# Attention with chunk selection and an MLP: preparing uniform blocks of 256 tokens over all eight heads, in wide instructions, instead of one head pair over the whole sequence

## The chip, the cores and the metric

One core of a Trainium2 chip runs the whole program. The metric is the device time of one execution in microseconds (us). The engines are named as the profile names them: PE (TensorE, matmuls; PEld is its weight load), DVE (VectorE), ACT (ScalarE), POOL (GpSimd) and SP (SyncE, which issues transfers). PSUM is the memory into which this program's matmuls write. SWDGE means the transfers that GpSimd issues, X the MLP's input for one block of tokens.

Every kernel was run beside the kernel before on the same chip, in rounds.

## The reference

Batch 4, 8 heads, 768 tokens, head size 64. Keys are cut into chunks of 32 tokens. For each query an upper bound of its score with every chunk is computed from the chunk's smallest and largest key per dimension; the best six chunks are kept, and causal softmax attention runs over those. Its output, 3072 tokens by 512, goes through an MLP with a softplus.

```python
k_min, k_max = k_chunks.min(axis=3), k_chunks.max(axis=3)
ub = sum(maximum(q * k_min, q * k_max), axis=-1)          # per query and chunk
top_chunks = argsort(where(causal, ub, -1e9))[..., -6:]
scores = where(selected & causal, scale * q @ k.T, -1e9)
attn_out = softmax(scores) @ v                            # 4 x 8 x 768 x 64
h = x @ w_in                                              # 3072x512 @ 512x2048
out = softplus(h) @ w_out                                 # 3072x2048 @ 2048x512
```

## The kernel before

The unit of preparation is a head pair over all 768 tokens, 16 of them. `prep_pair` transposes k and q on PE, reduces each chunk of keys to its maximum and minimum on DVE, computes the bounds `ub` on PE, takes the best of them with one MAX8 instruction per tile and head, and transposes the mask. It is a generator with four pieces, and a piece is emitted at certain slots of the attention of the pair before.

```python
kT = ps_t.tile([128, S], BF16, name="kT", tag="t")
for t in range(NQT): nc.tensor.transpose(kT[:, t*128:(t+1)*128], k_sb[:, t], ident)
nc.vector.tensor_reduce(kx[:, 0], kT3, axis=AX.X, op=ALU.max)     # 768 columns
nc.vector.tensor_reduce(kx[:, 1], kT3, axis=AX.X, op=ALU.min)
nc.scalar.copy(ka[0:64, :], kT[0:64, :]); nc.scalar.copy(kb[64:128, :], kT[64:128, :])
...                                                               # (cut) bd copies, on POOL later
PREP_AT = (0, 1, 4, 8)
for i in range(len(pairs)):                 # 4 batches x 4 head pairs
    nxt = prep_pair(i + 1)
    for blk in range(NBLK):                 # 3 blocks of 256 queries
        for _ in score_step(i, blk):        # 2, 4, 6 slots
            slot([nxt] if idx in PREP_AT else [])
```

A slot emits one score step (two matmuls `s_ps` and one exp `pt`), one step of the attention output that is waiting (`o_ps`, then `rec` and `o_sb` on DVE, which divide by the softmax sum, then the transpose `oT` and the copy into the MLP's input), and one piece of the MLP. The MLP's first matmul writes `hp`, ACT makes the softplus from it (`e_sb`, then `g`), and the second matmul writes `y`. A piece is 8 `hp` matmuls or 4 `y` matmuls, 0.87 us of PE. There is a single `o_ps` buffer in PSUM: the next pair's output can't start before DVE has read the last one.

```python
def av_step(i, blk, pt):
    o_ps = ps_o.tile([128, 2, 2, D + 1], F32, name="o_ps")        # ps_o: bufs=1
    ...
    nc.vector.reciprocal(rec, o_ps[:, :, :, D:D + 1])
    nc.vector.tensor_tensor(o_sb, o_ps[:, :, :, 0:D], rec.to_broadcast(...), op=ALU.mult)
```

The MLP of 256 tokens needs all four head pairs of that block. With this order of loops it becomes possible only in the fourth pair. The order within an engine is not the order of the text: the compiler's scheduler plans it.

The softmax here doesn't subtract the row's maximum and nothing guards it: scores larger than these inputs give would overflow.

Of the kernel before, what the change touches and what calls it, by code (L numbers as in the profile page):

```python
# [14 lines left out]
ACT = mybir.ActivationFunctionType  # L15


@with_exitstack
def kernel(
# [9 lines left out]
    nc = tc.nc  # L29
# [10 lines left out]
    NTOK = B * S  # L40
    KDM = d_model // 128
    KFF = d_ff // 128
    QB = 256
    NBLK = S // QB
    NK = 4
    NV = 5

    nc.scalar.preload_act_table_set("natural_log_exp_and_others")
# [3 lines left out]
    f_pool = ctx.enter_context(tc.tile_pool(name="f", bufs=4))  # L52
    io_pool = ctx.enter_context(tc.tile_pool(name="io", bufs=3))
    qt_pool = ctx.enter_context(tc.tile_pool(name="qt", bufs=4))
    prep = ctx.enter_context(tc.tile_pool(name="prep", bufs=2))
    pt_pool = ctx.enter_context(tc.tile_pool(name="pt", bufs=3))
    st_pool = ctx.enter_context(tc.tile_pool(name="st", bufs=3))
    g_pool = ctx.enter_context(tc.tile_pool(name="g", bufs=3))
# [7 lines left out]

    v_sb = [singles.tile([128, NQT, 2, D + 1], BF16, name=f"v_{i}") for i in range(NV)]
    KA = [singles.tile([128, S], BF16, name=f"ka_{i}") for i in range(NK)]
    KB = [singles.tile([128, S], BF16, name=f"kb_{i}") for i in range(NK)]
    w_in_sb = singles.tile([128, KDM, d_ff], BF16, name="w_in_sb")  # L70
    w_out_sb = singles.tile([128, KFF, d_model], BF16, name="w_out_sb")
    xT = [singles.tile([128, NTOK], BF16, name=f"xT_{p}") for p in range(NP)]

    pairs = [(b, p) for b in range(B) for p in range(NP)]
    loaded = {}

    def load_f32(i):
        for nm, x in (("k", k), ("q", q)):
            xf = f_pool.tile([128, NQT, 2, D], F32, name="xf")
            b, p = pairs[i]  # L80
            for h in range(2):
                nc.sync.dma_start(out=xf[:, :, h, :],  # L82
                                  in_=x[b, 2 * p + h].rearrange("(t s) d -> s t d", s=128))
            xb = io_pool.tile([128, NQT, 2, D], BF16, name=nm + "_sb")
            nc.scalar.copy(xb, xf)
            loaded[nm, i] = xb

    def load_cast(i):
        for nm, x in (("k", k), ("q", q)):
            xb = io_pool.tile([128, NQT, 2, D], BF16, name=nm + "_sb")  # L90
            b, p = pairs[i]
            for h in range(2):
                nc.gpsimd.dma_start(out=xb[:, :, h, :],  # L93
                                    in_=x[b, 2 * p + h].rearrange("(t s) d -> s t d", s=128))
            loaded[nm, i] = xb

    def load_v(i):
        b, p = pairs[i]
        for h in range(2):
            nc.gpsimd.dma_start(out=v_sb[i % NV][:, :, h, 0:D],  # L100
                                in_=v[b, 2 * p + h].rearrange("(t s) d -> s t d", s=128))
# [3 lines left out]
    load_f32(0)  # L105
    load_v(0)

    cmask = singles.tile([128, NQT, NCH], F32, name="cmask")
    nc.vector.memset(cmask, 0.0)
    nc.gpsimd.affine_select(out=cmask, in_=cmask, compare_op=ALU.is_ge, fill=-1.0e30,  # L110
                            base=0, channel_multiplier=1, pattern=[[128, NQT], [-CH, NCH]])
    ohb = singles.tile([32, S], BF16, name="ohb")
    nc.vector.memset(ohb, NEG)
# [6 lines left out]
    BD = [[singles.tile([128, 2, NCH], BF16, name=f"bd{m}_{i}") for m in range(2)]  # L120
          for i in range(2)]
    Mraw = [singles.tile([128, NQT, 2, 32], BF16, name=f"mraw_{i}") for i in range(2)]
    for i in range(2):
        for m in range(2):
            nc.vector.memset(BD[i][m], 0.0)
        nc.vector.memset(Mraw[i], 0.0)
    for i in range(NV):
        nc.vector.memset(v_sb[i][:, :, :, D:D + 1], 1.0)

    def init_k(i):  # L130
        nc.vector.tensor_copy(KA[i][64:96, :], ohb)
        nc.vector.memset(KB[i][0:32, :], 0.0)
        nc.vector.tensor_copy(KB[i][32:64, :], ohb)

    load_f32(1)
    load_v(1)
    for kt in range(KDM):
        nc.gpsimd.dma_start(out=w_in_sb[:, kt, :], in_=moe_w_in[kt * 128:(kt + 1) * 128, :])

    QA, QT, owner = {}, {}, {}  # L140

    def prep_pair(i):
        ka, kb = KA[i % NK], KB[i % NK]
        kmx, kmn = BD[i % 2]
        mraw = Mraw[i % 2]
        early = i < NP
        if i < NK:
            init_k(i)
        k_sb = loaded.pop(("k", i))
        q_sb = loaded.pop(("q", i))  # L150

        kT = ps_t.tile([128, S], BF16, name="kT", tag="t")
        for t in range(NQT):
            nc.tensor.transpose(kT[:, t * 128:(t + 1) * 128], k_sb[:, t], ident)  # L154
        kT3 = kT.rearrange("d (c g) -> d c g", g=CH)
        kx = prep.tile([128, 2, NCH], BF16, name="kx")
        nc.vector.tensor_reduce(kx[:, 0], kT3, axis=AX.X, op=ALU.max)  # L157
        nc.vector.tensor_reduce(kx[:, 1], kT3, axis=AX.X, op=ALU.min)
        nc.scalar.copy(ka[0:64, :], kT[0:64, :])
        nc.scalar.copy(kb[64:128, :], kT[64:128, :])  # L160
        eng = nc.vector if early else nc.gpsimd
        for m, dst in enumerate((kmx, kmn)):
            for h in range(2):
                eng.tensor_copy(dst[h * 64:(h + 1) * 64, h], kx[h * 64:(h + 1) * 64, m])
        owner["k", i % NK] = i
        yield

        qT = ps_t.tile([128, S], BF16, name="qT", tag="t")
        for t in range(NQT):
            nc.tensor.transpose(qT[:, t * 128:(t + 1) * 128], q_sb[:, t], ident)  # L170
        n = i + 2
        if n < len(pairs):
            if n < NP:
                load_f32(n)
            else:
                load_cast(n)
            load_v(n)
            owner["v", n % NV] = n
        if i == 1:
            for c4 in range(4):  # L180
                nc.gpsimd.dma_start(
                    out=w_out_sb[:, c4 * 4:(c4 + 1) * 4, :],
                    in_=moe_w_out[c4 * 512:(c4 + 1) * 512, :].rearrange(
                        "(kt ki) f -> ki kt f", ki=128))
        qt = qt_pool.tile([128, S], BF16, name="qt")
        qa = qt_pool.tile([128, S], BF16, name="qa")
        qpos = prep.tile([128, S], BF16, name="qpos")
        qneg = prep.tile([128, S], BF16, name="qneg")
        if early:
            nc.scalar.copy(qt, qT)  # L190
        else:
            nc.vector.tensor_copy(qt, qT)
        nc.vector.tensor_scalar_max(qpos, qt, 0.0)
        nc.vector.tensor_scalar_min(qneg, qt, 0.0)
        nc.vector.tensor_copy(qa[0:64, :], qt[0:64, :])
        QA[i], QT[i] = qa, qt
        yield

        ub = ps_t.tile([128, NQT, 2, NCH], F32, name="ub", tag="t")
        for t in range(NQT):  # L200
            ts = slice(t * 128, (t + 1) * 128)
            nc.tensor.matmul(ub[:, t], qpos[:, ts], kmx, start=True, stop=False)
            nc.tensor.matmul(ub[:, t], qneg[:, ts], kmn, start=False, stop=True)  # L203
        ub_sb = prep.tile([128, NQT, 2, NCH], F32, name="ub_sb")
        nc.vector.tensor_tensor(ub_sb, ub,
                                cmask.unsqueeze(2).to_broadcast([128, NQT, 2, NCH]), op=ALU.add)
        m8 = prep.tile([128, NQT, 2, 8], F32, name="m8")
        for t in range(NQT):
            for h in range(2):
                nc.vector.max(out=m8[:, t, h], in_=ub_sb[:, t, h])  # L210
        nc.vector.tensor_tensor(mraw[:, :, :, 0:NCH], ub_sb,
                                m8[:, :, :, TOPK - 1:TOPK].to_broadcast([128, NQT, 2, NCH]),
                                op=ALU.is_lt)
        nc.vector.tensor_copy(mraw[:, :, :, NCH:NCH + 1], m8[:, :, :, 0:1])
        yield

        mT = ps_t.tile([64, S], BF16, name="mT", tag="t")
        for t in range(NQT):
            nc.tensor.transpose(mT[:, t * 128:(t + 1) * 128], mraw[:, t], ident)  # L219
        nc.vector.tensor_copy(qa[64:96, :], mT[0:32, :])  # L220
        nc.vector.tensor_copy(qt[32:64, :], mT[32:64, :])
        yield

    later = deque()
    done = {}
    clock = [0]

    def score_step(i, blk):
        assert owner["k", i % NK] == i
        t0 = 2 * blk  # L230
        pt = pt_pool.tile([128, 2, NQT, QB], BF16, name="pt")
        for h in range(2):
            kk, rows, qq = ((KA[i % NK], 96, QA[i]), (KB[i % NK], 128, QT[i]))[h]
            for j in range(0, t0 + 2, 2):
                last = j == t0
# [37 lines left out]
    def ot_step(i, blk, o_sb):  # L273
        b, p = pairs[i]
        oT = ps_t.tile([128, QB], BF16, name="oT", tag="t")
        for u in range(2):
            nc.tensor.transpose(oT[:, u * 128:(u + 1) * 128], o_sb[:, u], ident)  # L277
# [62 lines left out]
    def slot(piece_gens=()):  # L340
        for g_ in piece_gens:
            next(g_, None)
# [55 lines left out]
```

## Time and profile before

The kernel takes 323.89 us (median of 3 runs, 323.69 to 324.35); the profiled execution spans 322.0 us.

From the page of the kernel before: the span in 40 slices of 8 us, the digit being the busy share in tenths, and the engines on the chain that ended last.

```profile
PE   1213788698999999899999999999999999999984
DVE  5543638957556657668474847484747321200010
ACT  2306756747997978868888888787879787566620
DMA  9999999909373929478392929100000000011001
PE 78%; ACT 7%; SPq 4%; DMA 4%; DVE 3%; issue 2%; POOL 1%; ACTq 0%; POOLq 0%
```

The DMA engines are full up to slice 8 (64 us). PE's digits are low up to 32 us and below nine in most slices up to 80 us (slice 10); from 80 us PE is full until the end. The windows view of the tile `hp` (the first MLP matmul) says it more exactly. Its columns are the stretch, its length, busy time and count of PE and of ACT, then the granted clock of PE (1.00 is full), the busy share of the DMA engines and GB/s.

```profile
0.00:40.00 40.00, 0.61 (x2) 0.00 (x0) 1.00 1.16 170
40.00:90.00 50.00, 9.00 (x67) 4.26 (x8) 0.83 1.01 81
90.00:278.00 188.00, 74.23 (x565) 42.49 (x71) 1.00 0.44 49
```

The MLP hardly exists before 80 us.

Busy time can't price pipelined matmuls (the record of an `hp` lasts 274 ns, but the next one ends 109 ns later), so I count differently, here and below. From the trace's records I take the step from one matmul's end to the next: 109 ns for 256 columns (`hp`), 216 ns for 512 (`y`), 56 ns for a 128-column transpose, 30 ns for `o_ps`, 25 ns for `ub`. The Trainium skill, "TensorE: Matmul & The Clock Gate", section "Wait — 56ns, not 53.3ns?", gives columns / 2.4 GHz plus about 2.5 ns on a warm array, and the first three agree. Steps times counts is 249.9 us of PE work. A stretch's length less the work that ended in it is PE time lost there:

| stretch of the kernel before, us | length | PE work | lost |
|---|---|---|---|
| 0 to 40 | 40 | 5.1 | 34.9 |
| 40 to 90 | 50 | 25.7 | 24.3 |
| 90 to 278 | 188 | 181.6 | 6.4 |
| 278 to 322 | 44 | 37.4 | 6.6 |

### The profile page before, as it was taken

Reading aid. Unit: us, or ns where it says so; the run is one execution under the profiler, and the core shown is the slowest. Engines: PE = TensorE matmul, PEld = TensorE weight load, DVE = VectorE, ACT = ScalarE, POOL = GpSimd, SP = SyncE. Lnnn points to the kernel's source line nnn. Section 1 sums busy time; section 2 is a strip of 40 time slices with the busy share of each in tenths; the row PEclk is TensorE's granted clock in tenths of the full one; section 3 lists DMA queues with packets and bytes.
Section 4 is the critical chain, followed back from the end, with each engine's and each line's share of the span. In section 5 each row is a group of like instructions: output and inputs, shape, how many; then the busy total and the mean of one; then the engine's idle time right before and its main releaser. Section 6 shows DMA issues by size and latency. Waiting matters only on the chain.

```text
span 322.0 us, 7075 instructions
## 1 busy us (share of the span) xinstructions
PE 278.0 (86%) x2784; PEld 203.4 (63%) x2784; DVE 167.9 (52%) x573; ACT 225.0 (70%) x381; POOL 123.9 (38%) x242
## 2 busy tenths in 40 slices
PE   1213788698999999899999999999999999999984
PEld 0102465485867777677777777777777777666631
DVE  5543638957556657668474847484747321200010
ACT  2306756747997978868888888787879787566620
POOL 8401688846444545558191919131212111000000
PEclk9999997857999999999999999999999999999999
DMA  9999999909373929478392929100000000011001
GB/s 151 197 193 184 128 185 106 91 7 70 26 51 49 92 20 88 59 53 85 38 83 44 99 43 71 38 35 34 2 35 35 34 2 35 33 63 37 33 35 67
DMA packets 81442, 21.96 MB, mean 68 GB/s; under 512 B 75776, under 2 KB 77824, under 8 KB 81408
## 3 DMA queue, kind: packets, MB, share of 16 engines
q0 software_dynamic: 65408, 12.06, 46.2%
q1 hardware_dynamic: 16000, 9.44, 10.6%
q8 instruction: 22, 0.36, 0.5%
q14 instruction: 12, 0.10, 0.1%
HBM read 27.26 MB, written 6.29 MB: 104 GB/s over the span
## 4 chain that ended last, share of the span: by engine, by line
PE 78%; ACT 7%; SPq 4%; DMA 4%; DVE 3%; issue 2%; POOL 1%; ACTq 0%; POOLq 0%
PE y L311 26%; PE hp L298 25%; PE o_ps L260 7%; PE s_ps L238 7%; PE s_ps L241 5%; SPq L82 4%; DMA xf<-in_q_dram 4%; ACT pt L243 3%; PE mT L219 3%; PE oT L277 2%; PE kT L154 2%; PE qT L170 1%; ACT e_sb L300 1%; DVE y_sb L316 1%; PE ub L203 1%
## 5 line engine op out<-in xcount | busy, mean ns | idle before, releaser
L243 ACT ACTIVATE pt<-s_ps 128x384 bf16<-128x384 f32 (+1 forms) x192 | 101.3, 548 | 30.0 <-PE s_ps L241 27.9
L311 PE MATMUL y<-w_out_sb,g 128*128 128x512 bf16 x384 | 98.2, 379 | 1.6 <-DVE y_sb L316 1.6
L247 POOL TENSOR_SCALAR_AFFINE_SELECT pt<-pt 128x256 bf16<-128x256 bf16 x96 | 40.1, 426 | 135.7 <-ACT pt L243 134.5
L298 PEld LDWEIGHTS <-w_in_sb 128*128 128x128 bf16 x768 | 70.7, 98 | 12.9 <-issue 1.2
L300 ACT ACTIVATE e_sb<-hp 128x512 f32<-128x512 f32 x96 | 57.5, 600 | 27.5 <-PE hp L298 26.7
L298 PE MATMUL hp<-xT_116,w_in_sb 128*128 128x256 bf16 x192 | 52.4, 274 | 0.8 <-ACT e_sb L300 0.8
L298 PE MATMUL hp<-xT_118,w_in_sb 128*128 128x256 bf16 x192 | 52.4, 274 | 0.0
L298 PE MATMUL hp<-xT_119,w_in_sb 128*128 128x256 bf16 x192 | 52.4, 273 | 0.0
L298 PE MATMUL hp<-xT_117,w_in_sb 128*128 128x256 bf16 x192 | 52.3, 273 | 0.0
L311 PEld LDWEIGHTS <-g 128*128 128x128 bf16 x384 | 34.4, 97 | 27.3 <-issue 2.1
L302 ACT ACTIVATE g<-e_sb 128x1024 bf16<-128x1024 f32 x48 | 50.9, 1060 | 0.4
L316 DVE COPY y_sb<-y 128x512 f32<-128x512 f32 x24 | 16.6, 692 | 51.6 <-PE y L311 51.5
L260 PEld LDWEIGHTS <-pt 128*128 128x128 bf16 x672 | 32.5, 103 | 4.4 <-issue 1.6
L157 DVE TENSOR_REDUCE kx<-kT 128x24 bf16<-128x768 bf16 x16 | 15.3, 958 | 20.6 <-PE kT L154 20.6
L93 POOL DMA_DIRECT2D k_sb<-in_k_dram x24 | 20.1, 839 | 7.1 <-PE kT L154 6.4
L93 POOL DMA_DIRECT2D q_sb<-in_q_dram x24 | 20.6, 861 | 0.8 <-issue 0.6
L154 PE MATMUL kT<-ident,k_sb 128*128 128x128 bf16 x96 | 9.3, 242 | 13.4 <-ACT kb_110 L160 7.1
L268 DVE TENSOR_TENSOR o_sb<-o_ps,rec 128x256 bf16<-128x256 f32 x48 | 20.1, 419 | 1.1
L266 DVE RECIPROCAL rec<-o_ps 128x4 f32<-128x4 f32 x48 | 8.4, 176 | 22.9 <-PE o_ps L260 22.6
L220 DVE COPY qa<-mT 32x768 bf16<-32x768 bf16 x16 | 8.8, 549 | 16.7 <-PE mT L219 16.6
L277 PE MATMUL oT<-ident,o_sb 128*128 128x128 bf16 x96 | 14.2, 232 | 2.0 <-DVE o_sb L268 2.0
L154 PEld LDWEIGHTS <-k_sb 128*128 128x128 bf16 x96 | 7.0, 109 | 13.7 <-issue 7.3
(171 smaller groups left out, 453.6 us busy)
## 6 DMA issues: line engine op xcount, KB each, us to landing
out_dram<-y_sb SPq DMA_DIRECT2D x24, 256.0 KB, 2.0
k_sb<-in_k_dram POOLq DMA_DIRECT2D x24, 96.0 KB, 3.1
q_sb<-in_q_dram POOLq DMA_DIRECT2D x24, 96.0 KB, 3.2
w_in_sb<-in_moe_w_in_dram POOLq DMA_DIRECT2D x4, 512.0 KB, 11.0
w_out_sb<-in_moe_w_out_dram POOLq DMA_DIRECT2D x4, 512.0 KB, 10.1
xf<-in_k_dram SPq DMA_DIRECT2D x8, 192.0 KB, 5.9
xf<-in_q_dram SPq DMA_DIRECT2D x8, 192.0 KB, 6.1
v_101<-in_v_dram POOLq DMA_DIRECT2D x8, 96.0 KB, 4.1
```

The lines of the kernel that those rows point to most:

```text
L93: nc.gpsimd.dma_start(out=xb[:, :, h, :], in_=x[b, 2 * p + h].rearrange("(t s) d -> s t d", s=128))
L154: nc.tensor.transpose(kT[:, t * 128:(t + 1) * 128], k_sb[:, t], ident)
L238: nc.tensor.matmul(s_ps[:, 0:QB], kk[0:rows, j * 128:(j + 1) * 128], qq[0:rows, t0 * 128:(t0 + 2) * 128], start=True, stop=True)
L243: nc.scalar.activation(pt[:, h, j:j + 2].rearrange("k j c -> k (j c)")[:, 0:n], s_ps[:, 0:n], ACT.Exp, scale=scale)
L247: nc.gpsimd.affine_select(out=diag, in_=diag, compare_op=ALU.is_ge, fill=0.0, base=0, channel_multiplier=-1, pattern=[[0, 2], [1, 128]])
L260: nc.tensor.matmul(o_ps[:, u, h], pt[:, h, j, c0:c0 + 128], v_sb[i % NV][:, j, h, :], start=(j == 0), stop=(j == t0 + u))
L268: nc.vector.tensor_tensor(o_sb, o_ps[:, :, :, 0:D], rec.to_broadcast([128, 2, 2, D]), op=ALU.mult)
L277: nc.tensor.transpose(oT[:, u * 128:(u + 1) * 128], o_sb[:, u], ident)
L298: nc.tensor.matmul(hp[:, fi], w_in_sb[:, dt, ft * 128:(ft + 1) * 128], xT[dt][:, cs], start=(dt == 0), stop=(dt == KDM - 1))
L300: nc.scalar.activation(e_sb[:, f2 * 2:f2 * 2 + 2], hp, ACT.Exp)
L302: nc.scalar.activation(g[:, f4 * 4:(f4 + 1) * 4], e_sb, ACT.Ln, bias=1.0)
L311: nc.tensor.matmul(y, g[:, f, u * 128:(u + 1) * 128], w_out_sb[:, f, :], start=(f == 0), stop=(f == KFF - 1))
```

## The change

The unit becomes a block of 256 tokens over all four head pairs, 12 of them. The same pieces handle 4 x 256 = 1024 columns at once, in single instructions, in four pieces at slots 0, 2, 5 and 9 of a period of 16 (slot 11 casts v in the first blocks and is empty in the others). Attention goes block by block, so the MLP of a block can follow its attention directly. Further: the first block's q, k and v are loaded first, by two queues; the weights are issued one transfer per score mask afterwards; in the start, and on POOL and SP for the whole kernel, the text's order is kept by hand (`manual_schedule`); the MLP gets 0, 0.8, 0.8 and then 1 piece per slot.

```diff
-        kT = ps_t.tile([128, S], BF16, name="kT", tag="t")
+        kT = ps_t.tile([128, NP, QB], BF16, name="kT", tag="t")      # 4 pairs x 256
...
-        nc.vector.tensor_reduce(kx[:, 0], kT3, axis=AX.X, op=ALU.max)
-        nc.vector.tensor_reduce(kx[:, 1], kT3, axis=AX.X, op=ALU.min)
-        nc.scalar.copy(ka[0:64, :], kT[0:64, :])
-        nc.scalar.copy(kb[64:128, :], kT[64:128, :])
+        nc.scalar.copy(kt, kT)
+        nc.vector.tensor_reduce(kx[:, :, 0], kT4, axis=AX.X, op=ALU.max)
+        nc.vector.tensor_reduce(kx[:, :, 1], kT4, axis=AX.X, op=ALU.min)
...
+        if not early:                                  # ka, kb now on DVE from block 3 on
+            nc.vector.tensor_copy(ka[0:64, :, cs], kt[0:64])
+            nc.vector.tensor_copy(kb[64:128, :, cs], kt[64:128])
...
-    PREP_AT = (0, 1, 4, 8)
+    PER = 16
+    for n in range(2, NB):
+        base = PER * (n - 1) - PER // 2
+        plan(n, ..., [base + o for o in (0, 2, 5, 9, 11)])
...
+    with tc.manual_schedule(engines={ET.Activation, ET.DVE, ET.PE}):
+        ...
+        run_block(0, 0.0)
+    run_block(1, 0.8)
+    for n in range(2, NB):
+        run_block(n, 1.0 if n > 2 else 0.8)
```

## The prediction

> **What bounds the kernel now.** Two stages. From about 80 us on it is TensorE: the windows view gives PE 195.6 busy of 198 us in 80 to 278 us, at full clock. Steps from one matmul's end to the next in the trace's records: 109 ns for a 256-column `hp` matmul, 216 ns for a 512-column `y`, 56 ns for a transpose, 30 ns for `o_ps`, 25 ns for `ub`. The first three agree with the Trainium skill, "TensorE: Matmul & The Clock Gate", Part 1, which gives columns / 2.4 GHz plus about 2.5 ns for a warm array. Multiplied by the counts, all PE work is about 249 us (MLP 166, scores 36, transposes 21.5, `o_ps` 20, `ub` 5). Of the 322 us span about 73 us are lost, and about 57 of them before 80 us: there PE does only some 23 us of such work. The `hp` tile's windows show 12 of 768 matmuls before 80 us, the `y` tile's none, because the MLP of the first 256 tokens needs all four head pairs, and each pair is prepared and attended over all 768 tokens first. There the DMA engines are full (tenths of 9).
>
> **What the change does.** PE counts are unchanged (2784 matmuls, the same of each kind), so the steady stage should not get cheaper. On DVE 385 program rows become 342, with the same elements; DVE is 52% busy and 3% of the chain: worth almost nothing. On ACT the two `ka`/`kb` copies per pair (about 0.79 us each, 25 us in all) become twelve `kt` copies of about 1.05 us (scaled from 0.79 for 768 columns), but batch 0 gains casts of k, q, v. ACT stays near 225 us.
>
> The gain is in order: block 0 prepares 256 tokens of all heads, so its MLP may start after 8 slots rather than after three full pairs.
>
> **Start, estimated.** Block 0's q, k arrive by about 8 us (the hardware queue moved about 2850 packets of 256 B in 4 us; k and q are 4096). Casts, transposes, copy, two reduces (about 1.2 us each), ub, 16 MAX8 (1.5), mask: first scores at 19 to 20 us, against 26.5. Block 0's 8 exps share ACT with block 1's preparation, about 15 us of ACT work: X of block 0 complete, and weights `w_in` landed, at 36 to 38 us; sustained `hp` from there, against 79 us. Block 1 is then ACT-bound (about 23 us), block 2 PE-bound (27): at about 87 us, batch 0's attention and 32 MLP pieces of 0.87 us (8 `hp` or 4 `y`) are done. Before, at 80 us, it is 1.5 pieces. So 30.5 x 0.87 = 26.5 us, less the 7 us later: 20 us. Then 200 us of PE work at about 4% loss (before: 198 us for 189 of work) and 5 us tail: span about 299, time about 301.
>
> **Predicted: 301 us, 8 in 10 between 291 and 311. Faster by over 2%: 0.94; within: 0.05; slower: 0.01.**
>
> **What would show it.** Right: `hp` groups sustained from below 42 us; PE tenths high from about slice 6; PE matmul count and step times unchanged; a chain made of `hp` and `y`. Wrong: MLP starting after 50 us; `hp` or `e_sb` waits on ACT in the steady stage; PE gaps at block borders, where the MLP stream says "wait"; a half-clock stretch after the MLP has begun.
>
> **What could break it.** Weights queue behind SWDGE issue on POOL; ACT's order stalls on a late cast; a tail of `hp` alone is ACT-bound (0.6 plus 0.53 us per 0.87).

## More of the kernel before

Where I say that an instruction stands behind another in an engine's queue, the engine's timeline shows it starting after that one although its own inputs were ready.

Lost time is not all idle time. By the records PE runs at half pace (transposes 107 ns apart instead of 56, `o_ps` 54 instead of 30) until 48 us, and again in 52 to 55, 62 to 72 and 76 to 79 us; from there it is at full pace, and the clock column says 1.00 for 90 to 278 us. Steps of about double length make up some 7.8 of the 24.3 us lost in 40 to 90 us.

Why the scores themselves begin late is in ACT's timeline (start, length, what, and in brackets the idle time before it and what ended it):

```profile
13.17 0.79 ACT L159 COPY ka_106<-kT 64x768 bf16<-64x768 bf16 x1
24.19 0.83 ACT L85 CAST q_sb<-xf 128x768 bf16<-128x768 f32 x1 [10.23 <-DMA xf<-in_q_dram]
...
30.23 0.87 ACT L243 ACTIVATE pt<-s_ps 128x384 bf16<-128x384 f32 x2
```

ACT stands for 10.23 us before a cast of the second pair's q, whose transfer has not landed; behind it in the queue wait the first pair's last copy and the first exp, at 30.2 us.

## The result and the profile after

The changed kernel takes 316.67 us (median of 4 runs, 315.70 to 317.26) against 324.12 for the kernel before in the same rounds: ratio 0.977, 95% interval 0.974 to 0.980. It is faster, but by a third of what was predicted, and outside the range. The profiled execution spans 314.1 us.

The same rows of the page after, whose slices are 7.9 us:

```profile
PE   1335879989899799899999799899999999999983
DVE  5818582592965964935946946836748732112100
ACT  4578789968837858788628868888539769983550
DMA  9999899993933906904913905907900000001101
PE 57%; DVE 26%; ACT 12%; issue 2%; DMA 1%; ACTq 0%; DVEq 0%
```

PE fills earlier, as meant. But in the middle its row is no longer all nines (records that the trace lacks, see below, take a part of that), and DVE is now on the chain that ended last with 26% of the span, against 3% before. `hp` in the windows view:

```profile
0.00:40.00 40.00, 0.63 (x2) 0.00 (x0) 1.00 1.09 188
40.00:90.00 50.00, 17.56 (x126) 9.93 (x16) 0.93 1.06 104
90.00:278.00 188.00, 74.24 (x552) 42.05 (x69) 1.00 0.47 50
```

126 `hp` matmuls lie in 40 to 90 us instead of 67. Lost PE time by my count, the kernel before beside it (the trace lacks 36 `y` records, which I restored from the program's order; without that the loss would be 7.8 us too high):

| stretch, us | lost before | lost after | difference |
|---|---|---|---|
| 0 to 40 | 34.9 | 32.0 | -2.9 |
| 40 to 90 | 24.3 | 10.3 | -14.0 |
| 90 to 278 | 6.4 | 14.9 | +8.5 |
| 278 to end | 6.6 | 6.9 | +0.3 |

The start gained 16.9 us. About 4 of the 14.0 us gained in 40 to 90 us are pace: after the change PE is at full pace from about 38 us, falls back once, from 41 to 47 us, and steps of about double length are some 3.5 of the 10.3 us lost in 40 to 90 us, against 7.8 of 24.3. Whether the earlier work brought the pace is not separated. The steady stage, 90 to 278 us, has the full clock in both kernels and gave 8.5 us back. The list of waits of PE in it (who waited for whom: total us, times, longest) is short before, and names only POOL:

```profile
PE ub L203 <- POOL bd_0_150 L164: 1.3, 1, 1.3
PE o_ps L260 <- POOL pt L247: 0.2, 1, 0.2
```

After, it names DVE:

```profile
PE o_ps L285 <- DVE o_sb L293: 3.0, 2, 1.5
PE oT L304 <- DVE o_sb L293: 2.7, 4, 1.2
PE hp L322 <- ACT e_sb L324: 1.5, 3, 0.5
PE y L335 <- DVE y_sb L340: 0.9, 2, 0.5
```

DVE's timeline at the first of those waits:

```profile
99.94 1.22 DVE L181 TENSOR_REDUCE kx<-kt 128x32 bf16<-128x1024 bf16 x1 [0.52 <-ACT kt L179]
101.08 1.21 DVE L182 TENSOR_REDUCE kx<-kt 128x32 bf16<-128x1024 bf16 x1
102.20 0.68 DVE L200 COPY qt<-qT 128x1024 bf16<-128x1024 bf16 x1
102.80 0.81 DVE L184 COPY bd_113<-kx 64x64 bf16<-64x64 bf16 x2
103.62 0.69 DVE L203 TENSOR_SCALAR qpos<-qt 128x1024 bf16<-128x1024 bf16 x1
104.23 0.87 DVE L204 TENSOR_SCALAR qneg<-qt 128x1024 bf16<-128x1024 bf16 x1
105.02 0.16 DVE L291 RECIPROCAL rec<-o_ps 128x4 f32<-128x4 f32 x1
105.10 0.86 DVE L237 COPY qa<-qt 64x1024 bf16<-64x1024 bf16 x1
105.89 0.40 DVE L293 TENSOR_TENSOR o_sb<-o_ps,rec 128x256 bf16<-128x256 f32 x1
```

The last `o_ps` matmul of a pair ends at 101.86 us by the records. Its reciprocal `rec` starts at 105.02 and `o_sb` ends at 106.3, 4.4 us after the matmul (the quickest pair takes 0.68 us), because one block's preparation stands in front of it without a gap: two reduces over 1024 columns, `qt`, `bd`, `qpos`, `qneg`. PE meanwhile stands in front of the next `o_ps`:

```profile
106.35 0.35 PE L285 MATMUL o_ps<-v_107,pt 128*128 128x65 bf16 x6 [1.50 <-DVE o_sb L293]
```

The kernel before has the same burst, but it is shorter and it finds PE elsewhere:

```profile
101.36 0.96 DVE L157 TENSOR_REDUCE kx<-kT 128x24 bf16<-128x768 bf16 x1 [0.84 <-PE kT L154]
102.23 0.95 DVE L158 TENSOR_REDUCE kx<-kT 128x24 bf16<-128x768 bf16 x1
103.09 0.55 DVE L192 COPY qt<-qT 128x768 bf16<-128x768 bf16 x1
...
104.24 0.34 DVE L195 COPY qa<-qt 64x768 bf16<-64x768 bf16 x1
105.44 0.18 DVE L266 RECIPROCAL rec<-o_ps 128x4 f32<-128x4 f32 x1 [0.86 <-PE o_ps L260]
105.65 0.42 DVE L268 TENSOR_TENSOR o_sb<-o_ps,rec 128x256 bf16<-128x256 f32 x1
```

Its six instructions from `kx` to `qa` take 3.2 us, and DVE is idle when the attention output arrives. Over all pairs after 90 us, the time from the last `o_ps` matmul to the end of `o_sb` is at most 2.05 us before, and over 2 us in one pair of 36; after, it is up to 4.45 us and over 2 us in 7 of 37.

### The profile page after: what moved, and what is told of

It is laid out like the page before. It is cut to its first block, busy times and chain, and to the rows that moved or that the text cites. A ratio compares the mean times of both kernels' runs of the same rounds, so it can differ in the third digit from the quotient of the medians.

```text
span 314.1 us, 6878 instructions
## 1 busy us (share of the span) xinstructions
PE 270.5 (86%) x2748; PEld 198.6 (63%) x2784; DVE 174.4 (56%) x550; ACT 224.2 (71%) x379; POOL 99.0 (32%) x172
## 4 chain that ended last, share of the span: by engine, by line
PE 57%; DVE 26%; ACT 12%; issue 2%; DMA 1%; ACTq 0%; DVEq 0%
PE y L335 21%; PE hp L322 17%; PE o_ps L285 5%; PE s_ps L263 4%; DVE kx L181 4%; ACT kt L179 4%; DVE kx L182 4%; PE s_ps L265 3%; PE mT L236 3%; ACT pt L267 2%; DVE qneg L204 2%; ACT e_sb L324 2%; DVE qpos L203 2%; DVE qt L200 2%; DMA xf<-in_k_dram 1%
## 5 line engine op out<-in xcount | busy, mean ns | idle before, releaser
L267 ACT ACTIVATE pt<-s_ps 128x512 bf16<-128x512 f32 (+1 forms) x192 | 103.9, 556 | 36.7 <-PE s_ps L265 29.9
L322 PE MATMUL hp<-x,w_in_sb 128*128 128x256 bf16 x768 | 103.5, 273 | 3.2 <-ACT e_sb L324 1.8
L335 PE MATMUL y<-w_out_sb,g 128*128 128x512 bf16 x348 | 90.7, 379 | 3.6 <-DVE y_sb L340 1.7
L285 PEld LDWEIGHTS <-pt 128*128 128x128 bf16 x672 | 32.9, 99 | 11.1 <-issue 4.3
L340 DVE COPY y_sb<-y 128x512 f32<-128x512 f32 x24 | 16.5, 687 | 39.7 <-PE y L335 39.5
L305 DVE COPY x<-oT 128x256 bf16<-128x256 bf16 x48 | 13.9, 289 | 25.1 <-PE oT L304 24.8
L285 PE MATMUL o_ps<-v_106,pt 128*128 128x65 bf16 x336 | 20.7, 199 | 2.2 <-DVE o_sb L293 1.9
L181 DVE TENSOR_REDUCE kx<-kt 128x32 bf16<-128x1024 bf16 x12 | 14.6, 1219 | 13.0 <-ACT kt L179 13.0
L285 PE MATMUL o_ps<-v_107,pt 128*128 128x65 bf16 x336 | 18.4, 193 | 1.7 <-DVE o_sb L293 1.5
L114 POOL DMA_DIRECT2D k_sb<-in_k_dram x18 | 16.1, 892 | 0.8 <-issue 0.5
L114 POOL DMA_DIRECT2D q_sb<-in_q_dram x18 | 16.2, 902 | 0.4 <-issue 0.3
L263 PE MATMUL s_ps<-qt,kb_110 128*128 128x256 bf16 x48 | 14.0, 293 | 1.6 <-ACT pt L267 0.9
L263 PE MATMUL s_ps<-qa,ka_108 96*128 96x256 bf16 x48 | 14.2, 296 | 0.8 <-DVE qa L241 0.8
```

Source lines behind the costliest of these rows:

```text
L114: nc.gpsimd.dma_start(out=xb[:, t], in_=rows(nm, n, t))
L181: nc.vector.tensor_reduce(kx[:, :, 0], kT4, axis=AX.X, op=ALU.max)
L263: nc.tensor.matmul(s_ps[:, 0:QB], kk[0:nr, p, j * 128:(j + 1) * 128], qq[0:nr, p, :], start=True, stop=True)
L267: nc.scalar.activation(pt[:, h, j:j + 2].rearrange("k j c -> k (j c)")[:, 0:w], s_ps[:, 0:w], ACT.Exp, scale=scale)
L285: nc.tensor.matmul(o_ps[:, u, h], pt[:, h, j, c0:c0 + 128], V[b % 2][:, j, 2 * p + h, :], start=(j == 0), stop=(j == t0 + u))
L322: nc.tensor.matmul(hp[:, fi], w_in_sb[:, dt, ft * 128:(ft + 1) * 128], X[n][:, dt], start=(dt == 0), stop=(dt == KDM - 1))
```

## The experiments

Theory A: the preparation's burst on DVE, now about a quarter longer per instruction (1.22 against 0.96 us for a reduce) and with more of them, stands ahead of the normalisation in DVE's queue, and PE waits for it. Theory B: the loss comes from the MLP's order at block borders and from ACT; DVE only looks late. Theory C: the scheduler's plan, built with modelled durations, puts PE in front of results that are not there. Theory D: GpSimd's issues of block loads slow DVE's instructions. About the start there is a question of its own: how much is the early MLP worth?

All runs are of rounds with the kernel before; its medians there were 323.2 to 324.2 us.

| run | median us | ratio to before | lost 0-40 | 40-90 | 90-278 | 278-end |
|---|---|---|---|---|---|---|
| changed kernel | 316.67 | 0.977 | 32.0 | 10.3 | 14.9 | 6.9 |
| no_reduce (other work) | 304.93 | 0.942 | 31.8 | 7.4 | 6.9 | 6.6 |
| double_reduce | 319.84 | 0.988 | 33.5 | 13.0 | 15.5 | 5.7 |
| split | 311.34 | 0.962 | 32.0 | 9.6 | 10.4 | 6.9 |
| hold_mlp | 318.85 | 0.985 | 32.0 | 17.1 | 11.8 | 7.5 |
| manual | 349.37 | (slow runs) | 33.5 | 16.5 | 36.3 | 11.3 |
| manual_double | 374.62 | 1.159 | 34.5 | 22.3 | 48.6 | 18.4 |
| no_swdge (wrong result) | 310.99 | 0.963 | 32.9 | 9.7 | 9.6 | 6.9 |
| finer | 307.00 | 0.950 | 32.0 | 9.6 | 8.1 | 5.7 |
| finer_hold | 315.89 | 0.976 | 32.0 | 18.3 | 8.2 | 6.2 |
| finer_dve | 306.50 | 0.947 | 31.6 | 9.2 | 8.4 | 5.6 |
| finer_dve_vpool | 306.36 | 0.947 | 30.9 | 7.9 | 8.3 | 5.5 |
| weights_first | 320.15 | 0.991 | 33.2 | 11.0 | 17.3 | 6.8 |
| finer_later2 | 306.17 | 0.947 | 31.7 | 5.6 | 11.6 | 5.9 |
| all_later2 | 305.06 | 0.943 | 30.8 | 5.9 | 11.2 | 5.7 |

### The two reduces dropped: no_reduce

```diff
-        nc.vector.tensor_reduce(kx[:, :, 0], kT4, axis=AX.X, op=ALU.max)
-        nc.vector.tensor_reduce(kx[:, :, 1], kT4, axis=AX.X, op=ALU.min)
+        nc.vector.tensor_copy(kx[:, :, 0], kT4[:, :, :, 0])
+        nc.vector.tensor_copy(kx[:, :, 1], kT4[:, :, :, 1])
```

> Wrong result on purpose: the two 1.2 us chunk reduces of each block become copies of 32 elements, everything else and all dependences stay. Theory A (a burst of block-wide DVE instructions stands in DVE's queue ahead of the normalisation of the attention output, and TensorE waits for that): about 2.2 us less DVE ahead of it per block, nine steady blocks, so 5 to 9 us faster than the changed kernel (308 to 312 us), and the TensorE stalls over 60 ns between 90 and 278 us fall from some 14 us to under 8. Theory B (the loss is in the MLP order at block borders and in ACT, DVE only looks late): under 2 us.

It takes 304.93 us, 11.7 us less than the changed kernel, more than theory A's upper edge. The steady loss falls from 14.9 to 6.9 us, the level of the kernel before, and the waits for `o_sb` are almost gone:

```profile
PE s_ps L263 <- ACT pt L267: 0.6, 2, 0.3
PE o_ps L285 <- DVE o_sb L293: 0.3, 2, 0.2
```

So theory A's effect is there, and theory B falls as the main cause of the steady loss. Another 2.9 us came in 40 to 90 us. This kernel selects chunks by bounds that are wrong, and the comparison with the reference still passed it: with these inputs the comparison does not see which chunks are taken, so a pass says little about the selection.

### The two reduces doubled: double_reduce

```diff
+        nc.vector.tensor_reduce(kx[:, :, 0], kT4, axis=AX.X, op=ALU.max)
+        nc.vector.tensor_reduce(kx[:, :, 1], kT4, axis=AX.X, op=ALU.min)
```

> Right result: each of the two chunk reduces is issued twice, 2.3 us more DVE per block, 28 us in all. Theory A: at least half of it in the nine steady blocks shows, 8 to 20 us slower than the changed kernel (325 to 337 us). Theory B (DVE, 56 percent busy, has room): under 3 us slower.

It takes 319.84 us, only 3.2 us more, and the steady loss is the same, 15.5 us. That is near theory B's number and against theory A's. Yet its normalisations take up to 5.71 us from the last `o_ps` matmul, against 4.45: a longer hold costs no more by itself, it depends on what PE finds to do meanwhile. PE and DVE have another order in this trace, so I take it that the scheduler planned around the longer burst. The run does not test A alone, which is why manual_double was made.

### The text's own order, with single and with doubled reduces: manual, manual_double

```diff
-    run_block(1, 0.8)
-    for n in range(2, NB): ...
+    with tc.manual_schedule(engines={ET.Activation, ET.DVE, ET.PE}):
+        run_block(1, 0.8)
+        for n in range(2, NB): ...              # and the rest, to the end
```

> Right result: TensorE, ScalarE and VectorE keep the order of the program text to the end, as the changed kernel does for block 0 only; no compiler reordering. It tells whether the reordering, which plans with modelled durations, puts TensorE in front of results that the vector engine has not got to (theory C: 3 to 9 us faster than the changed kernel, steady stalls under 9 us), or whether the order as written is worse (over 2 us slower: then the reordering was hiding latency).

> Right result: the run named manual with each chunk reduce issued twice. With the order fixed nothing can be rearranged around the longer burst, so theory A (the burst ahead of the normalisation holds TensorE) now expects at least 10 us over manual, where the doubled reduces under the reordering cost only 3 us. If it again costs under 4 us, the vector engine's burst does not hold TensorE and the gain of dropping the reduces came another way.

Manual took 343.9 us once and 349.3 to 349.6 three times; its profile is of a slow run, so I use it roughly. It is far slower than the scheduler's order: theory C falls in the form in which I put it. Manual_double takes 374.62 us, 25 us over manual's median (of slow runs) and 31 over its one fast run, for 28 us of added DVE work. That is over the 10 us that theory A asked for, but not all of it is waiting: before the tail, PE stands at half clock for 41 us in the profile of manual_double and for 20 us in that of manual. The 20 us more at half clock can be worth 10 us at most, by my estimate. So with the order fixed the doubling does cost time, how much is not measured apart; that the scheduler's order hid it in double_reduce is likely, not shown.

### The burst cut, the work the same: split and finer

Split cuts the preparation of batches 1 to 3 from four pieces into ten in slots of their own, with the same wide instructions (the recorded text says eleven: the last slot is empty). Finer also halves each reduce, which makes twelve.

```diff
-            nc.vector.tensor_reduce(kx[:, :, 0], kT4, axis=AX.X, op=ALU.max)
-            nc.vector.tensor_reduce(kx[:, :, 1], kT4, axis=AX.X, op=ALU.min)
+            for m, op in enumerate((ALU.max, ALU.min)):              # finer; blocks 3 to 11
+                for g in range(0, NP, 2):
+                    nc.vector.tensor_reduce(kx[:, g:g + 2, m], kT4[:, g:g + 2], axis=AX.X, op=op)
+                    if m == 0 or g == 0:
+                        yield
...                                    # a yield also before qpos, qneg, ka, kb and the mask copies
-        plan(n, ..., [base + o for o in (0, 2, 5, 9, 11)])
+        plan(n, ..., [base + o for o in (0, 1, 2, 3, 4, 5, 6, 7, 9, 10, 11, 12, 13)])
```

> Right result: in the nine blocks of batches 1 to 3 the preparation is cut from 5 pieces into 11, one or two wide DVE instructions per slot, at slots 0 to 13 of a block; the instructions are the same. Theory A: the normalisation gets between them, 2 to 7 us faster than the changed kernel (310 to 315 us). Theory B: no change within 1 us.

> Right result: as split, and each chunk reduce cut in two halves of two head pairs (about 0.65 us), in slots of their own. Theory A: as fast as split or up to 3 us faster (308 to 312 us); if the count of vector instructions mattered more than their length, slower than split.

Split takes 311.34 us and finer 307.00, correct, with nothing removed: 5.3 and 9.7 us less than the changed kernel, finer past the range expected. The steady loss falls to 10.4 and 8.1 us. No normalisation after 90 us takes over 1.61 us any more in finer. Its DVE timeline in a stretch of the same stage:

```profile
99.05 2.46 DVE L187 TENSOR_REDUCE kx<-kt 128x16 bf16<-128x512 bf16 x4 [0.51 <-ACT kt L179]
101.43 0.17 DVE L305 RECIPROCAL rec<-o_ps 128x4 f32<-128x4 f32 x1
101.55 0.44 DVE L191 COPY bd<-kx 64x64 bf16<-64x64 bf16 x2
102.02 0.42 DVE L307 TENSOR_TENSOR o_sb<-o_ps,rec 128x256 bf16<-128x256 f32 x1
...
103.90 0.69 DVE L207 COPY qt<-qT 128x1024 bf16<-128x1024 bf16 x1 [0.40 <-PE qT L198]
104.51 0.17 DVE L305 RECIPROCAL rec<-o_ps 128x4 f32<-128x4 f32 x1
104.71 0.48 DVE L212 TENSOR_SCALAR qpos<-qt 128x1024 bf16<-128x1024 bf16 x1
105.11 0.41 DVE L307 TENSOR_TENSOR o_sb<-o_ps,rec 128x256 bf16<-128x256 f32 x1
105.44 0.41 DVE L215 TENSOR_SCALAR qneg<-qt 128x1024 bf16<-128x1024 bf16 x1
```

The four half reduces still lie side by side here, but `rec` and `o_sb` get in between the rest, and PE's wait for `o_sb` in 90 to 278 us is now:

```profile
PE o_ps L299 <- DVE o_sb L307: 0.6, 3, 0.2
```

This is what theory A says, shown with the right result and the same amount of work: the stretch of DVE work without a break was the cost, not the work. The longest normalisation after 90 us and the steady loss fall together: 4.45 and 14.9 us in the changed kernel, 2.81 and 10.4 in split, 1.61 and 8.1 in finer, 1.90 and 6.9 in no_reduce, 2.05 and 6.4 in the kernel before. Two limits: the pieces carry matmuls too, and PE's order in finer is another, so what the order alone is worth is not isolated; and about 2 us of finer's gain lie outside the steady stage, in part because its profile has half the clock for 3.4 us in 40 to 90 us and the changed kernel's for 6.8.

### No block loads: no_swdge

```diff
-        loads.append(chain(*(load_cast(nm, n) for nm in "kqv")))
+        loaded["k", n], loaded["q", n] = fixed["k"], fixed["q"]      # block 0's, again
...                                    # V of odd batches set to ones; one staging buffer fewer
```

> Wrong result on purpose: from block 3 on no q, k, v is loaded; block 0's q and k and an all-ones v are used again. GpSimd issues no block loads and the DMA engines are idle but for outputs. Theory D (bf16 vector instructions are slowed by GpSimd's DMA issues, 0.43 to 0.7 or 0.9 us in the profile, and that makes the burst long): 3 to 8 us faster than the changed kernel and qpos, qneg, ka, kb back at 0.43 us. Otherwise within 1.5 us.

It takes 310.99 us, 5.7 us less, with the relative error of 0.52 that was meant. Most of the lengthened DVE instructions came back to their shorter length (`qneg`, `qa`, `ka`, `kb`, `bd`), but not `qpos`. From the groups of instructions (count, busy us, mean ns), the changed kernel and then this one:

```profile
L204 DVE TENSOR_SCALAR qneg<-qt 128x1024 bf16<-128x1024 bf16 x12 | 7.8, 652 | 0.0
```

```profile
L208 DVE TENSOR_SCALAR qneg<-qt 128x1024 bf16<-128x1024 bf16 x12 | 5.2, 436 | 0.0
```

652 ns became 436 ns on average, with the same instruction. The Trainium skill, "SBUF — State Buffer", section "Who interferes with whom", says that VectorE in its two-port modes and GpSimd hold a shared port pair in turns, and that copies and `tensor_scalar` can be in such a mode while `tensor_reduce` can't. The traces agree: the reduces are 1214 ns with and without the loads. So theory D is a part of theory A: the burst is also long because GpSimd issues loads into it. The run takes away the transfers as well, so by its time alone it does not separate the port from the DMA traffic. `qpos` says a little more. It is the same operation on the same shape, and its mean stays at 492 and 491 ns: without any block load three of its twelve instances still take 672 to 675 ns, each beside a score mask on GpSimd (a fourth beside a mask takes 426, most of the others 426 to 428). A GpSimd instruction is enough there, without a load.

### What the early MLP is worth: hold_mlp, finer_hold

```diff
-    run_block(1, 0.8)
+    run_block(1, 0.0)
...
-        run_block(n, 1.0 if n > 2 else 0.8)
+        run_block(n, 1.0 if n > 2 else 0.0)
```

> Right result: the MLP is not started until batch 0's attention is issued (rate 0 in blocks 1 and 2), as in the kernel before; block-wise preparation stays. If the gain of the change is the early MLP start, some 24 MLP pieces of 0.87 us go from the time before 87 us to the end, where TensorE has no idle time to hide them: 13 to 20 us slower than the changed kernel, so slower than the kernel before too (329 to 337 us). If the gain came from cheaper preparation instead, it stays below 322 us.

> Right result: the run finer with the MLP held back as in hold_mlp, to price the early MLP start without the vector engine's stalls in the steady stage. If the early MLP start were worth what the prediction gave it (some 13 of the 20 us of the start), this is over 318 us. If batch 0's attention is bound by ScalarE, so that MLP pieces put there only lengthen it, the early start is worth 2 to 7 us: 309 to 314 us.

Hold_mlp takes 318.85 us, 2.2 us more than the changed kernel, not 13 to 20. On top of finer the same edit costs 8.9 us (315.89 against 307.00), between the two expectations. Counting pieces in the records shows why the price is not 0.87 us each. At the start of batch 1's attention the changed kernel has done 24.2 pieces at 86.7 us; hold_mlp has done 8.6 (the scheduler pulled some forward although the text did not ask for them) at 77.6 us. The 15.6 extra pieces are 13.6 us of PE work, but they made batch 0's attention 9.1 us longer, which leaves 4.5 us; and hold_mlp's steady stage lost 3.1 us less than the changed kernel's. PE's idle time in the start is not free room. A part of the price is pace: in 40 to 90 us finer_hold has half the clock for 10.2 us and finer for 3.4, and steps of about double length cost it some 3 us more.

### ScalarE in the start: finer_dve, finer_dve_vpool

Both move copies of blocks 1 and 2 (and, in the second, the casts of v) from ACT to DVE and POOL.

```diff
-        if early:
+        if n == 0:
             nc.scalar.copy(qt, qT)
...                                    # ka, kb and the mask rows likewise; v cast by nc.gpsimd in the second
```

> Right result: finer, and blocks 1 and 2 take their four copies (qt, ka, kb, the mask rows; about 4.1 us of ScalarE each) on the vector engine, as later blocks do. If ScalarE bounds the stretch from 17 to 60 us: 2 to 6 us faster than finer (301 to 305 us). If the vector engine's chain bounds it: no gain, or slower.

> Right result: finer_dve, and the six casts of v in blocks 0 to 2 (0.57 us of ScalarE each) on GpSimd. If ScalarE still bounds: 1 to 3 us faster than finer_dve. GpSimd may issue the weights later behind them: then none.

Finer_dve takes 306.50 us, against 307.00: not the 2 to 6 us expected if ScalarE bounds the start, though ACT is 18.9 of 20 us busy from 40 to 60 us in the changed kernel. The median of finer_dve_vpool, 306.36, hides two kinds of execution: 304.47 us twice at a mean clock of 0.99, and 308.2 and 308.3 at 0.98. The difference in clock, 1.3% of 306 us, is by itself an estimated 4 us, as much as lies between them. At finer_dve's clock it is thus 2.0 us faster than finer_dve, as expected if ScalarE still bounds; with four executions that fall so far apart the run decides nothing.

### The weights early: weights_first

```diff
-        loads.append(load_w_in())                       # one transfer per score mask
+    for half in range(2): ...                           # all eight right after POOL's constants
```

> Right result: the changed kernel with the eight loads of w_in issued right after GpSimd's constants at about 5 us, as the kernel before does, instead of one after each score mask from 20 us. If holding the weights back is what brings the first scores from 26.5 to 17 us: first exp 3 to 8 us later and 1 to 5 us slower than the changed kernel (318 to 322 us). If not: within 1 us or faster, as the MLP finds its weights sooner.

It takes 320.15 us, 3.5 us more, within the range. The reason I gave is wrong, though: the first scores begin at 16.9 us, as in the changed kernel. The loss is 0.7 us more in 40 to 90 us, 1.2 more in 0 to 40 and 2.4 more in 90 to 278 us. Of those 2.4 us up to 1.7 can be a half-clock stretch of 3.4 us from 110 us on, which the changed kernel's profile does not have. Holding weights back is thus worth something in these runs, how much is uncertain, but the earlier first scores come from elsewhere: in the changed kernel ACT has no cast of a later block in front of the first exp (19.2 us instead of 30.2 us). I did not isolate that by an experiment.

### The missing pieces: finer_later2, all_later2

I had reckoned 32 MLP pieces by the end of batch 0's attention. Following the text by hand shows 25: only one waiting output step is emitted per slot, so the first 256 tokens are complete at slot 17 and not at slot 8, and pieces asked for earlier are dropped. The trace has 24.2. These runs ask for the missing ones.

```diff
-        if later and later[0][0] <= clock[0]: ...
+        for _ in range(2 if clock[0] < 40 else 1):
+            if later and later[0][0] <= clock[0]: ...
...
-    run_block(1, 0.8)
+    run_block(1, 1.0)                                   # and block 2
```

> Right result: finer, with two steps of the waiting attention outputs per slot in the first 40 slots and rate 1.0 instead of 0.8 in blocks 1 and 2, so the program's order has 32 MLP pieces by the end of batch 0's attention instead of 25. If each early piece saves its 0.87 us as the prediction reckoned: 6 us faster than finer (301 us). From the price of holding the MLP back (9 us for 16 pieces, 0.55 us each): 2 to 4 us faster (303 to 305 us). If that stretch has no room: no gain.

> Right result: finer_later2 with the ScalarE relief of finer_dve_vpool. If ScalarE is what bounds the start once more pieces are there: 2 to 4 us faster than finer_later2. If not: within 1 us of it.

The records now show 32.5 pieces at 86.9 us, which is the prediction's picture of the start almost to the number, and the loss in 40 to 90 us falls from 9.6 to 5.6 us. Yet the time is 306.17 us, 0.8 less than finer's. The gain is given back at once. The `hp` windows of this run:

```profile
86.00:94.00 8.00, 0.98 (x6) 0.00 (x0) 1.00 1.08 95
```

In 8 us only six `hp` matmuls: the MLP has caught up with attention and waits for block 2's tokens, whose last copy into its input ends at 94.1 us. From the first score of block 3 to the first of block 4 the pieces go from 32.5 to 32.8. The steady loss rises from 8.1 to 11.6 us, 2.4 of it in 90 to 100 us. The MLP cannot run ahead of attention, so pieces done earlier were taken from what would have filled PE a little later. All_later2 adds the relief of ACT: 305.06 us, 1.1 us less than finer_later2, at the edge of "within 1 us".

All_later2 has the lowest median of the correct versions here, 0.943 of the kernel before (95% interval 0.940 to 0.946), and most of its gain over the changed kernel is finer's.

## Why the prediction was wrong

The direction was right, though at a ratio of 0.977 only just by over 2%; the size was not. The sum was: 20 us gained in the start, a steady stage as before, 301 us. The measured time is 316.67. Of the 15 us between the predicted span of 299 us and the measured 314.1, 8.5 are the steady stage and 3.1 the start; about 3 lie in the sum itself, as 322 less 20 is 302.

1. **"PE counts are unchanged ..., so the steady stage should not get cheaper", and then "about 4% loss (before: 198 us for 189 of work)".** This is the step that failed most: the steady stage's loss was carried over. The counts are unchanged, but the loss is not a property of the counts. It went from 6.4 to 14.9 us in 90 to 278 us, by a wait that the prediction did not have: PE for `o_sb`, which stands behind the preparation in DVE's queue. No_reduce, split, finer and no_swdge, four different ways to shorten or break DVE's burst, bring it to 6.9, 10.4, 8.1 and 9.6 us.
2. **"DVE is 52% busy and 3% of the chain: worth almost nothing."** The share says that DVE has room, not when. One run of preparation without a break holds up a normalisation of 0.68 us behind it by up to 3.8 us, and PE's single `o_ps` buffer turns that into idle PE. The prediction listed waits of the steady stage on ACT and on block borders as what could go wrong; waits on DVE were not in the list.
3. **"32 MLP pieces ... are done" at 87 us.** 24.2 were done at 86.7 us. This was a misreading of the program, not of the hardware: the waiting outputs pass one step per slot. finer_later2 has the 32 pieces and is only 0.8 us faster, so as a cause of the miss it is small.
4. **"30.5 x 0.87 = 26.5 us, less the 7 us later: 20 us."** Measured, the start up to 90 us gained 16.9 us. That it came so near is partly luck: with 24 pieces instead of 32, and with about 3 us net from the pace of PE up to 90 us, which the prediction did not reckon with. A piece done early is not worth its 0.87 us: 8.9 us for some 16 pieces on top of finer.
5. **First scores "at 19 to 20 us, against 26.5".** Right in kind, a little cautious: 17.0 us.
6. **Sustained `hp` "at 36 to 38 us".** The sustained stretch begins at about 47 us. Of the four copies into the first block's MLP input the second, at 39.8 us, stands behind two reduces of block 2 on DVE, and the last, at 45.6 us, behind block 2's MAX8 instructions and mask: the same kind of wait as in 1, already in the start. The half clock named among the signs of a wrong prediction lies there too, from 40.5 to 47.3 us.
7. **PE matmuls and step times unchanged.** Right. The chain "made of `hp` and `y`" was not: DVE had 26% of it.

The cause of the steady loss is shown: shortening or breaking the burst in four ways takes away 4.5 to 8.0 of the 8.5 us. What stays open is what exactly bounds the stretch from 17 to 60 us. Taking four copies per block from ACT brings 0.5 us, the casts of v as well gives 304.5 or 308.3 us with the clock, more MLP pieces alone are given back, all together bring 2 us. I did not find one cause.

## What to carry to other kernels

In this kernel, merging narrow instructions into wide ones saved little on an engine with room (DVE is busy for 168 us before and for 174 after, with some copies that other engines had before), and it lengthened the stretch in which that engine served nobody else: look at the longest run of instructions ahead of the short one that the bounding engine waits for, not at busy shares. If a batch of background work must be done, cut it into parts about as long as the wait that its neighbours can bear, and give each its own place. Before reckoning what work moved earlier is worth, follow the program's own order to see when its inputs exist, and ask what fills the place that it leaves.

## What the Trainium skill lacked or had wrong

- "TensorE: Matmul & The Clock Gate", section "Back-to-back issue gap", says that a stream of weight load and matmul pairs runs at about 81 ns per matmul of 128 columns and about 131 ns for 512 columns. Here each matmul has its own weight load, and the trace shows 56 ns (`oT` transposes) and 216 ns (`y`): the page's formula for the isolated gap fits, its "sustained" figures do not.
- "SBUF — State Buffer", section "Who interferes with whom", has the exclusion of GpSimd and two-port VectorE instructions, but no cost in a kernel with frequent block loads from GpSimd's queue. Here the mean of `qneg` over 1024 columns was 652 ns with them and 436 ns without.
- No page that I found says what a long run of VectorE instructions does to a short one queued behind it that PE waits for. Here most of 8.5 us of 314 went that way: up to 4.45 us from the last matmul of an attention output to its normalised copy, against at most 1.61 us once the run was cut.
